# Attention and mixture-of-experts kernel: the scheduler's clock of a unit's row steps is moved on by one microsecond ahead of their transposes

## The chip, the cores and the metric

The kernel runs on one core of a Trainium2 chip. The metric is the device time of one execution in microseconds (us). The engines are TensorE (PE, with PEld for its weight loads), VectorE (DVE), ScalarE (ACT), GpSimd (POOL) and SyncE (SP), which here does nothing but issue transfers.

## The reference

Two layers follow each other. The first is a local attention over 7 taps with weights from a softmax; its output, 8 x 3584 = 28672 tokens of 192 numbers, goes into a layer with 8 experts of which each token takes one:

```python
w = exp(w - max(w)); w = w / (sum(w) + 1e-9)          # over the 7 taps, 8 heads
out[b, s, h] = sum_k w[b, s, h, k] * x_pad[b, s + k, h]   # x shifted by 0 to 6 tokens

logits = x @ w_gate                                   # x: 28672 x 192
e_idx = argmax(logits, axis=1)
gate_w = softmax(logits)[n, e_idx]
eom = sigmoid(x @ w_output_gate)
for e in range(8):
    h = maximum(x[mask_e] @ w1[e], 0)                 # 192 -> 1024
    out[mask_e] = gate_w * eom[:, e] * (h @ w2[e])    # 1024 -> 192
```

## The kernel before

The tokens are cut into 32 *units* of 896 (a batch has four; 128 partitions with 7 tokens each). A unit goes through a front:

- SP loads its weights `w` and its tokens `x` (for the first unit of a batch also the `halo`, the tokens shifted). There are four buffers for x.
- POOL and DVE multiply the taps (`gap`, `vt`), DVE adds them up.
- `sum_steps` turns the sums into rows `rt` in two half-precision parts (high and low), on ACT and DVE. There are three such row buffers.
- SP issues seven DMA transposes that turn `rt` into `gt`, the only buffer of its kind.
- PE multiplies `gt` by the gate's weights `gm` (21 small matmuls, "the logits"). DVE reduces them (`lz`), finds each token's expert (`eq`, `fm`) and counts with a scan (`p3`). PE turns that into ranks with two small matmuls, `p3` by `upper` and by ones. DVE works out each row's place `posi`.
- POOL scatters the rows by indirect DMA to their places in a table `srtd` in memory, sorted by expert (seven issues, `srtd<-rt,posi`).

As soon as an expert has enough rows, *tiles* are cut from the table: T0 to T75, with 512, 384, 256 or 128 rows of one expert. `round_steps` makes the list of tiles of each unit (tile 42 is one of unit 25), and from unit 31 on the remaining tiles are mixed by size. For each tile SP issues five loads (`tile_load`): `meta`, the transposed rows `xT`, two pieces of `wa` (the first layer's weights) and `wb` (the second's). A load that reads `srtd` waits for the scatters of all units up to its own. Then PE runs gemm1, five matmuls for each of its units of 512 columns (`ps<-xT,wa`), ACT makes `hh` (the high half of the activations), DVE `hl` (the low half), PE runs gemm2 for each group of 128 rows, 24 matmuls (`ps<-wb,hh` and `ps<-wb,hl`), ACT scales into `ys`, and POOL scatters `ys` to the output (`out_dram<-ys,meta`).

The order on each engine is fixed when the program is built, by a planner. Each step sequence, such as a unit's `sum_steps` or the loads of a tile, is a `Chain` with a reckoned time `c.t`: the earliest time at which its next instruction can start. `Order.step` always takes the chain whose start would be earliest, the latest of three times:

```python
at = max(self.now, c.t - c.slack, c.engine.t - c.engine.lead)
key = (at - c.favour, c.rank)
```

Between equal times the rank decides. The engines are modelled by `Paced` (each instruction moves the engine's clock and the chain's time by a cost and a latency) and the SP queue by `Queue`. The planner's times only set the order: on the chip every engine works through its own list and waits by semaphores. An instruction that waits holds up what stands behind it on the same engine, the SP queue too.

The steps that the change touches are in `sum_steps`, behind the split of the rows: from unit 5 on (`TR_U`), the chain takes the one buffer `gt`, issues the transposes on the queue `TQ` (SP), and goes on with the logits. The tile loads compete with these transposes for the places in SP's list.

Of the kernel before, what the change touches and what calls it, by code (L numbers as in the profile page):

```python
# [48 lines left out]
def SIZES(u, last):  # L49

    if last:
        return ((512, 0), (256, 0), (128, 0))
    return EARLY.get(u, ((512, 0),))

# [178 lines left out]
def kernel(ctx: ExitStack, tc: tile.TileContext, x, wg, wgate, wogate, w1, w2, cst, out):  # L233
    nc = tc.nc
    od = Order()
# [38 lines left out]
    def take(slots, engine):  # L274

        yield engine, lambda: slots
        got = slots.pop(0)
        od.cur.t = max(od.cur.t, got[0] if isinstance(got, tuple) else got)
        yield engine
        return got  # L280

    def take_place(slots):

        yield T_, lambda: slots or ("banks" in state and bank_free)
        got = slots.pop(0) if slots else (*bank_free.pop(0), bank_free)
        od.cur.t = max(od.cur.t, got[0])
        yield T_
        return got[1], got[2] if len(got) > 2 else slots
# [146 lines left out]
    def scales(ssq, sc, inv, name, free=None):  # L435

        n = ssq.shape[1]
        ex = f_ex if n == 2 else sp.tile([P, n], I32, tag=f"ex{n}", name=f"ex_{name}")
        V.tensor_scalar(ex, ssq.bitcast(I32), 1, MASK, op0=ALU.arith_shift_right, op1=ALU.bitwise_and)
        if free is not None:  # L440
            free.append(od.cur.t)
        yield V
        V.tensor_scalar(sc.bitcast(I32), ex, -1.0, float(197 << 23), op0=ALU.mult, op1=ALU.add)
        V.tensor_scalar(inv.bitcast(I32), ex, float(57 << 23), None, op0=ALU.add)
# [198 lines left out]
    def acc_steps(u, taps):  # L643
# [8 lines left out]
        while own or left:  # L652
# [25 lines left out]
            first = acc  # L678
        d["total"] = acc
        od.add(sum_steps(u), (RANK_B, u), S)  # L680

    def used(u, tag):
# [32 lines left out]
    def sum_steps(u):  # L715

        d = U[u]
        _, ri = yield from take(rt_free, S)
        d["ri"], rt = ri, ri.bitcast(F16)
        ssq = sp.tile([P, 1], F32, tag="ssq", name=f"ssq{u}")  # L720
        a3 = d["total"].rearrange("p (j h) g -> p j (h g)", h=H)

        b, q = u // UB, u % UB
        S.activation(ri[:, :, 192:194], tok.unsqueeze(2).broadcast_to([P, JS, 2]), AF.Copy, bias=float(b * SEQ + q * JS))
        S.activation(rt.bitcast(BF16)[:, :, 0:D], a3, AF.Square, accum_out=ssq)
        yield V
        sx = sp.tile([P, 1], F32, tag="sx", name=f"sx{u}")
        isx = d["isx"] = sp.tile([P, 1], F32, tag="isx", name=f"isx{u}")
        yield from scales(ssq, sx, isx, f"x{u}")
        yield S  # L730
        S.activation(rt[:, :, 0:D], a3, AF.Copy, scale=sx)
        yield V
        V.scalar_tensor_tensor(out=rt[:, :, 192:256], in0=a3[:, :, 128:192], scalar=sx, in1=rt[:, :, 128:192], op0=ALU.mult, op1=ALU.subtract)
        yield V
        V.scalar_tensor_tensor(out=rt[:, :, 256:384], in0=a3[:, :, 0:128], scalar=sx, in1=rt[:, :, 0:128], op0=ALU.mult, op1=ALU.subtract)
        d["split"] = True
        if u >= PE_U:
            acc_free.append(od.cur.t)
        else:
            sum_free.append((od.cur.t, d["sum_at"]))  # L740
        if u >= TR_U:
            yield from take(gt_free, TQ)
            gt = rp.tile([P, JS, 3, P], F16, tag="gt", bufs=GT, name=f"gt{u}")
            for j in range(JS):
                TQ.dma_start_transpose(out=gt[:, j], in_=rt[:, j, 0:384])
        yield S, lambda: "isg" in gates
        for k in ("isl", "nisl"):
            d[k] = sp.tile([P, 1], F32, tag=k, name=f"{k}{u}")
            S.activation(d[k], isx, AF.Copy, scale=gates[k[:-1] + "g"])
        yield T_  # L750
        at, home = yield from take_place(lg_free)
        lg = ps[:, at : at + 224].rearrange("p (j c) -> p j c", c=32)
        if u < TR_U:
            yield from pe_logits(u, rt, lg)
        else:
            od.cur.t += LAT_T
            for j0 in range(0, JS, 2):
                yield T_
                for j in range(j0, min(j0 + 2, JS)):
                    logits(lg, j, gt[:, j].rearrange("p k r -> p (k r)"))  # L760
            gt_free.append(od.cur.t)

        lz = d["lz"] = sp.tile([P, JS, 16], F32, tag="lz", name=f"lz{u}")
        yield V
        V.tensor_reduce(out=lz, in_=lg.rearrange("p j (h c) -> p j c h", h=2), axis=AX, op=ALU.add)
        home.append((od.cur.t, at))
        yield V

        l8 = lz[:, :, 0:8]
        yield from take(few_free, V)  # L770
        m = f_m
        V.tensor_reduce(out=m, in_=l8, axis=AX, op=ALU.max)
        yield V
        eq = sp.tile([P, JS, 8], F32, tag="eq", name=f"eq{u}")
        mb = m.unsqueeze(2).broadcast_to([P, JS, 8])
        V.tensor_tensor(out=l8, in0=l8, in1=mb, op=ALU.subtract)
        ex = d["ex"] = sp.tile([P, JS, 8], F32, tag="exl", name=f"exl{u}")
        od.add(exp_steps(u, ex, l8), (RANK_B, u), S)
        yield V
        V.scalar_tensor_tensor(out=eq, in0=l8, scalar=0.0, in1=e8b, op0=ALU.is_equal, op1=ALU.mult)  # L780
        yield V
        fm = sp.tile([P, JS], F32, tag="fm", name=f"fm{u}")
        V.tensor_reduce(out=fm, in_=eq, axis=AX, op=ALU.min)
        yield V
        ohe = f_oh
        oh = d["oh"] = ohe.rearrange("p e j -> p j e")
        V.tensor_tensor(out=oh, in0=e8b, in1=fm.unsqueeze(2).broadcast_to([P, JS, 8]), op=ALU.is_equal)
        yield V

        p3e = sp.tile([P, 8, JS], F16, tag="p3", name=f"p3_{u}")  # L790
        p3 = d["p3"] = p3e.rearrange("p e j -> p j e")
        V.tensor_tensor_scan(out=p3e.rearrange("p e j -> p (e j)"), data0=segs, data1=ohe.rearrange("p e j -> p (e j)"), initial=0.0, op0=ALU.mult, op1=ALU.add)
        od.cur.t += LAT_R
        yield T_
        d["rk_at"], d["rk_home"] = yield from take_place(rk_free)
        rk = d["rk"] = ps[:, d["rk_at"] : d["rk_at"] + 16]
        T_.matmul(rk[:, 0:8], lhsT=upper, rhs=p3[:, JS - 1, :], start=True, stop=True)
        T_.matmul(rk[:, 8:16], lhsT=ones16, rhs=p3[:, JS - 1, :], start=True, stop=True)
        od.add(weight_of_steps(u), (RANK_C, u, 1), V, V.t)
        od.add(place_steps(u), (RANK_C, u, 0), V)  # L800

    def logits(lg, j, gx):
        for k, m in enumerate(gates["mm"]):
            T_.matmul(lg[:, j, :], lhsT=gx[:, k * P : (k + 1) * P], rhs=m, start=(k == 0), stop=(k == 2), skip_group_check=True)

    def pe_logits(u, rt, lg):

        gx = None
        yield from take(gt_free, S)
        gt = rp.tile([P, JS, 3, P], F16, tag="gt", bufs=GT, name=f"gt{u}").rearrange("p j k r -> p j (k r)")  # L810
        for g0 in range(0, JS + 2, 2):
            for g in range(2):
                j = g0 - 2 + g
                if gx is not None and j < JS:
                    logits(lg, j, gt[:, j])
            ng = min(2, JS - g0)
            if ng > 0:
                yield from take(tr_free, T_)
                pt = turn
                for g in range(ng):  # L820
                    for k in range(3):
                        T_.transpose(out=pt[:, g * 384 + k * 128 : g * 384 + (k + 1) * 128], in_=rt[:, g0 + g, k * 128 : (k + 1) * 128], identity=ident)
                yield S
                gx = True
                S.copy(gt[:, g0 : g0 + ng, 0:384], pt[:, 0 : ng * 384].rearrange("p (j c) -> p j c", c=384))
                tr_free.append(od.cur.t)
                yield T_
        gt_free.append(od.cur.t)
        U[u]["turned"] = True

    def exp_steps(u, ex, l8):
        S.activation(ex, l8, AF.Exp, scale=U[u]["isl"])
        U[u]["exp"] = True
        U[u]["exp_t"] = od.cur.t
        return
        yield
# [314 lines left out]
    def last_turn_steps():  # L1151

        yield T_, lambda: state["weights"] == NE and "turned" in U[TR_U - 1]
        yield from take(tr_free, T_)
# [166 lines left out]
TURN_SP = True  # L1321
GT = 1
TR_U = 5
EARLY = {2: ((256, 0),), 4: ((384, 0),), 5: ((384, 0),), 6: ((384, 0),)}
EVERY = {*range(99)}
MANUAL = ("SP", "DVE", "PE", "Activation", "Pool")
# [18 lines left out]
```

## Time and the profile before

| | |
|---|---|
| median of 3 runs | 1253.18 us |
| lowest and highest | 1252.49 and 1254.74 us |
| profiled execution | 1240.45 us |
| its span in the trace | 1238.7 us |
| mean granted clock of PE | 0.985 |
| idle time of PE | 107.5 us (52.4 up to 300 us, 46.9 from 300 to 1000, 0.8 from 1000 to 1200, the rest at the end) |

The span is what the trace covers; the profiled execution is 1.7 us longer than it, and 12.7 us shorter than the median of the runs without a profile. A row of the timeline has the start and the duration in us, the engine, the source line, the operation with output and inputs and their shapes, and a count where equal instructions that follow each other are put together; in brackets stands the time that the engine stood idle before it and what ended that. Line 167 and line 139 are those of helpers through which every instruction goes, so all compute instructions show L167 and all issues of SP L139. The names in rows lack the numbers of units and tiles; which unit a row belongs to comes from its place in the order.

### The profile page before, as it was taken

The page shows a single profiled execution, that of the slowest core. Times are in us where ns is not written, and L with a number is a line of the kernel's source. Part 1 is how long each engine was busy: PE and PEld are TensorE (multiplying, and loading weights), DVE is VectorE, ACT ScalarE, POOL GpSimd, SP SyncE. Part 2 cuts the span into 40 slices and gives each one's busy share as a digit, 9 for nine tenths or more (in the row PEclk, how much of TensorE's full clock was granted, in tenths as well). Part 3 has the DMA queues.
Part 4 walks back from the last instruction along what each step waited for, and adds up shares of the span by engine and source line. Part 5 has one row for each costly group of instructions (what it writes and reads, how often), then busy time and mean ns, then how long its engine had stood idle before and what let it go on. Part 6 is the DMA issues. An engine that isn't in the chain of part 4 may idle for free.

```text
span 1238.7 us, 27551 instructions
## 1 busy us (share of the span) xinstructions
PE 1131.2 (91%) x9692; PEld 816.7 (66%) x9692; DVE 950.8 (77%) x2011; ACT 583.9 (47%) x1253; POOL 855.6 (69%) x759
## 2 busy tenths in 40 slices
PE   8987788798989999999999999999999999999997
PEld 4443357666666666766666666666666666888987
DVE  6787959988899899988988989989988753333331
ACT  2865634454444445544444544445444433444442
POOL 6676787886777888888878878878878654322222
PEclk9998899999999999999999999999999999999999
DMA  9885699799996787787857885986977496889991
GB/s 300 270 262 179 225 262 232 210 273 245 248 254 167 229 207 195 214 238 222 232 172 206 220 222 161 252 220 175 230 196 209 136 243 201 236 256 298 311 300 57
DMA packets 279404, 277.61 MB, mean 224 GB/s; under 512 B 213670, under 2 KB 238743, under 8 KB 279264
## 3 DMA queue, kind: packets, MB, share of 16 engines
q1 hardware_dynamic: 257424, 231.25, 67.8%
q0 software_dynamic: 21696, 44.30, 12.4%
q8 instruction: 76, 1.25, 0.4%
q14 instruction: 64, 0.52, 0.1%
q10 hardware_dynamic: 144, 0.29, 0.1%
HBM read 174.87 MB, written 60.28 MB: 190 GB/s over the span
## 4 chain that ended last, share of the span: by engine, by line
PE 54%; DVE 20%; issue 9%; POOL 6%; DMA 3%; SPq 2%; ACT 1%; another core or an unknown queue 1%; DVEq 0%; POOLq 0%; ACTq 0%
PE ps L167 54%; DVE ps L167 9%; DVE hl L167 5%; POOL gap L167 2%; POOL srtd L167 2%; SPq L139 1%; DVE vt L167 1%; DVE rt L167 1%; POOL out_dram L167 1%; DMA wb<-wd 1%; DMA wa<-wd 1%; DVE vap L167 1%; ACT hh L167 1%; DVE lz L167 0%
## 5 line engine op out<-in xcount | busy, mean ns | idle before, releaser
L167 PE MATMUL ps<-xT,wa 128*128 128x512 f16 (+3 forms) x2440 | 489.2, 347 | 32.9 <-DVE hl L167 13.6
L167 PE MATMUL ps<-wb,hh 128*128 128x192 f16 x3648 | 473.8, 247 | 13.8 <-issue 7.0
L167 PE MATMUL ps<-wb,hl 128*128 128x192 f16 x1824 | 450.6, 247 | 2.6 <-issue 2.6
L167 DVE SCALAR_TENSOR_TENSOR hl<-ps,hh 128x512 f16<-128x512 f32 (+1 forms) x470 | 306.1, 664 | 181.8 <-ACT hh L167 123.7
L167 POOL DMA_INDIRECT out_dram<-ys,meta x220 | 218.3, 992 | 235.1 <-ACT ys L167 174.5
L167 POOL TENSOR_TENSOR gap<-x,w 128x768 f32<-128x768 f32 (+5 forms) x251 | 343.4, 1392 | 38.6 <-PE ps L167 13.8
L167 PEld LDWEIGHTS <-wa 128*128 128x128 f16 x2440 | 226.7, 98 | 216.8 <-issue 44.8
L167 PEld LDWEIGHTS <-hh 128*128 128x128 f16 x3648 | 332.0, 98 | 54.9 <-issue 18.4
L167 ACT ACTIVATE hh<-ps 128x512 f16<-128x512 f32 (+1 forms) x470 | 269.3, 582 | 183.5 <-PE ps L167 151.4
L167 POOL DMA_INDIRECT srtd<-rt,posi x224 | 223.3, 997 | 80.3 <-issue 60.2
L167 ACT ACTIVATE ys<-ps,sc 128x192 f32<-128x192 f32 x228 | 95.6, 419 | 302.4 <-PE ps L167 188.1
L167 PEld LDWEIGHTS <-hl 128*128 128x128 f16 x1824 | 179.2, 98 | 3.8 <-issue 3.5
L167 DVE TENSOR_TENSOR ps<-ps,gap 128x1344 f32<-128x1344 f32 x116 | 179.8, 1550 | 0.7 <-POOL gap L167 0.4
L167 PE MATMUL ps<-gap,cf 128*128 128x512 f32 x168 | 72.9, 573 | 7.5 <-DVE ps L167 4.9
L167 POOL TENSOR_TENSOR gap<-halo,w 128x1152 f32<-128x1152 f32 (+4 forms) x37 | 59.4, 1606 | 17.2 <-PE ps L167 8.4
L167 DVE SCALAR_TENSOR_TENSOR rt<-ps,sx,rt 128x448 f16<-128x448 f32 x64 | 57.4, 909 | 10.2 <-ACT rt L167 3.1
L167 PE MATMUL ps<-vap,cf 128*128 128x512 f32 (+1 forms) x126 | 56.3, 583 | 3.4 <-DVE vap L167 3.4
L167 PEld LDWEIGHTS ps<-gap,cf 128*128 128x128 f32 x168 | 31.8, 201 | 39.2 <-issue 30.6
L167 DVE TENSOR_TENSOR vt<-x,ps 128x1344 f32<-128x1344 f32 (+2 forms) x42 | 52.7, 1269 | 0.2
L167 DVE TENSOR_TENSOR ps<-ps,vt 128x1344 f32<-128x1344 f32 x34 | 52.8, 1552 | 0.0
L167 PE MATMUL ps<-xT,late 128*128 128x128 f16 (+2 forms) x560 | 52.1, 250 | 0.5 <-issue 0.5
L167 ACT ACTIVATE rt<-ps,sx 128x1344 f16<-128x1344 f32 x32 | 44.0, 1375 | 10.7 <-DVE isx L167 5.4
(125 smaller groups left out, 815.0 us busy)
## 6 DMA issues: line engine op xcount, KB each, us to landing
wb<-wd SPq DMA_DIRECT2D x75, 768.5 KB
wa<-wd SPq DMA_DIRECT2D x61, 768.0 KB
x<-in_x_dram SPq DMA_DIRECT2D x32, 672.0 KB
late<-wd SPq DMA_DIRECT2D x14, 768.0 KB
wa<-wd SPq DMA_DIRECT2D x61, 128.0 KB
w<-in_wg_dram SPq DMA_DIRECT2D x32, 196.0 KB
wd<-wpb SPq DMA_DIRECT2D x8, 768.5 KB
st<-in_w_dram SPq DMA_DIRECT2D x8, 768.0 KB
```

Source lines behind the costliest of these rows:

```text
L139: r = f(*args, **kwargs)
L167: r = f(*args, **kwargs)
```

## The change

When a chain of `sum_steps` (unit 5 or later) has split its rows, its reckoned time is put 1.0 us later before it asks for the `gt` buffer and issues the transposes. The later steps of the same chain (scales on ACT, logits, ranks) are reckoned from that time too. A chain that competes for SP, the loads of a tile or of the next unit's tokens, comes first in SP's list if its time lies within that microsecond.

```diff
         if u >= TR_U:
+            od.cur.t += TURN_LAG
             yield from take(gt_free, TQ)
             gt = rp.tile([P, JS, 3, P], F16, tag="gt", bufs=GT, name=f"gt{u}")
             for j in range(JS):
                 TQ.dma_start_transpose(out=gt[:, j], in_=rt[:, j, 0:384])
...
 TR_U = 5
+TURN_LAG = 1.0
```

The number of instructions stays the same on every engine. The lists of PE, DVE and POOL are word for word the same (but for running numbers of buffers) for units 13 to 23; they differ in two stretches, about units 9 to 12 and units 24 to 31.

The first stretch begins on SP at the transposes of unit 9 (`gt9`). In these rows `w12`, `x12` and `halo` are the loads of unit 12, `ti6_0` is the list of unit 6's tiles, and `meta10` the first load of tile 10. Before:

```order
L139 DMA x11_3223<-in_x_dram 128x1344
L139 DMA w12_3272<-in_wg_dram 128x392
L139 DMA_TRANSPOSE gt9_3278<-rt_0_99 128x3x128 x7
L139 TENSOR_LOAD ti6_0_2421
L139 ISA x2
L1043 ISA
L139 DMA meta10_3441<-srtd_78 128x3x2
```

And after:

```order
L139 DMA x11_3223<-in_x_dram 128x1344
L139 DMA w12_3272<-in_wg_dram 128x392
L139 DMA halo_83<-in_x_dram 112x1152
L139 DMA halo_83<-in_x_dram 15x1152
L139 DMA x12_3280<-in_x_dram 128x1344
L139 DMA_TRANSPOSE gt9_3344<-rt_0_99 128x3x128 x7
L139 TENSOR_LOAD ti6_0_2421
```

The three loads of unit 12 have moved from behind tile 11's loads to ahead of `gt9`. On PE the logits of unit 9 have moved behind 34 more matmuls (ten of gemm1 of tile 9, 24 of gemm2 of tile 8), while the rank matmuls of unit 9 stand where they stood; those of unit 10 stand 29 matmuls later.

The second stretch shows first on DVE and PE at the ranks of unit 25. On DVE, `eq25`, `fm25` and `p3_25` are the search for the expert and the scan, `w27` and `w28` belong to the softmax of later units, and `hl38_0` is the low half of the first gemm1 unit of tile 38. Before:

```order
L167 TENSOR_TENSOR lz25_11751<-lz25_11751,ps_82 128x7x8
L167 TENSOR_TENSOR w27_10818<-w27_10818,ps_82 128x56x5
L167 SCALAR_TENSOR_TENSOR eq25_11814<-lz25_11751,ps_82 128x56
L167 TENSOR_TENSOR ps_82<-w27_10818,ps_82 128x112
L167 TENSOR_REDUCE fm25_11846<-eq25_11814 128x7
L167 TENSOR_REDUCE ps_82<-w28_11254 128x56
L167 TENSOR_TENSOR ps_82<-ps_82,fm25_11846 128x7x8
L167 TENSOR_TENSOR w28_11254<-w28_11254,ps_82 128x392
L167 SCALAR_TENSOR_TENSOR p3_25_11855<-segs_133,ps_82 128x56
L167 TENSOR_SCALAR ex_x26_11860<-ssq26_11807 128x1
L167 SCALAR_TENSOR_TENSOR hl38_0_11789<-ps_82,hh38_0_11788 128x512
```

And after:

```order
L167 TENSOR_TENSOR w27_10818<-w27_10818,ps_82 128x56x5
L167 TENSOR_TENSOR lz25_11750<-lz25_11750,ps_82 128x7x8
L167 SCALAR_TENSOR_TENSOR hl38_0_11789<-ps_82,hh38_0_11788 128x512
L167 SCALAR_TENSOR_TENSOR eq25_11816<-lz25_11750,ps_82 128x56
L167 TENSOR_TENSOR ps_82<-w27_10818,ps_82 128x112
L167 TENSOR_REDUCE fm25_11848<-eq25_11816 128x7
L167 TENSOR_REDUCE ps_82<-w28_11255 128x56
L167 TENSOR_TENSOR ps_82<-ps_82,fm25_11848 128x7x8
L167 TENSOR_TENSOR w28_11255<-w28_11255,ps_82 128x392
L167 SCALAR_TENSOR_TENSOR p3_25_11864<-segs_133,ps_82 128x56
```

`hl38_0` has moved ahead of the seven operations from `eq25` to `p3_25`. On PE the two rank matmuls of unit 25 have moved behind five more gemm1 matmuls of tile 38 and now stand in front of a gemm2 group of tile 37, not in the middle of tile 38's pair. The rank matmuls of unit 30 have moved in the same way, behind 34 matmuls: from the middle of a pair of gemm1 units of tile 46 to the middle of a pair of tile 47.

The third place is SP at the transposes of unit 27 (`gt27`). `x30` is the load of unit 30, `ti25_0` the list of unit 25's tiles, and `meta42`, `xT42`, `wa2` and `wb42` are the loads of tile 42. Before:

```order
L139 DMA x30_12292<-in_x_dram 128x1344
L139 DMA_TRANSPOSE gt27_12436<-rt_0_99 128x3x128 x7
L139 TENSOR_LOAD ti25_0_11989
L139 ISA x2
L1043 ISA
L139 DMA meta42_12594<-srtd_78 128x4x2
L139 ISA
L139 DMA_TRANSPOSE xT42_12596<-srtd_78 128x3x512
```

And after:

```order
L139 DMA meta42_12485<-srtd_78 128x4x2
L139 ISA
L139 DMA_TRANSPOSE xT42_12487<-srtd_78 128x3x512
L139 ISA
L139 DMA wa2_140<-wd_79 128x1536
L139 ISA
L139 DMA wa2_140<-wd_79 64x512
L139 ISA
L139 DMA wb42_12491<-wd_79 128x1537
L139 DMA_TRANSPOSE gt27_12593<-rt_0_99 128x3x128 x7
```

All five loads of tile 42 have moved ahead of `gt27`; in the same way those of tile 43 have moved ahead of the loads `w31` and `x31`, and those of tile 49 ahead of `gt31`. On PE the logits of unit 27 stand 68 matmuls later (48 of gemm2, 20 of gemm1), those of unit 29 58 later and those of unit 31 78 later. Among the tiles cut after the last unit, the sizes follow each other in another order: tile 52 is now one of 512 rows of unit 30 instead of one of unit 31's small ones; the number of 128-row blocks is the same.

## The prediction

> **What bounds the kernel now.** I read the page's engine line first, then windows of 50 us, and last the waits of the whole run, because a change of order can only pay where an engine waits.
>
> ```profile
> span 1238.7 us, 27551 instructions
> PE 1131.2 (91%) x9692; PEld 816.7 (66%) x9692; DVE 950.8 (77%) x2011; ACT 583.9 (47%) x1253; POOL 855.6 (69%) x759
> ```
>
> TensorE (PE) is busy for 1131.2 of 1238.7 us. So 107.5 us of PE idle time are all that a better order could take, with the little that half clock adds. The next rows are windows (length, then busy time of PE, PEld, DVE, ACT and POOL, then the granted clock, the DMA share and GB/s).
>
> ```profile
> 300.00:350.00 50.00, 46.67 (x404) 34.01 (x403) 45.68 (x111) 24.92 (x59) 38.08 (x33) 0.99 1.10 260
> 800.00:850.00 50.00, 45.63 (x388) 32.46 (x388) 43.12 (x78) 23.37 (x52) 40.41 (x37) 0.97 0.77 205
> 950.00:1000.00 50.00, 45.71 (x386) 31.91 (x385) 35.78 (x76) 22.26 (x51) 32.93 (x32) 1.00 0.51 135
> 1100.00:1150.00 50.00, 50.00 (x558) 43.31 (x557) 16.50 (x25) 20.84 (x44) 11.72 (x12) 1.00 0.94 264
> ```
>
> The front (units and tiles side by side) leaves PE 3 to 4 us idle in each 50, the late tiles none: 50.00 of 50.00. So the end is PE's work plus PE's waits in the front, and a microsecond of PE wait saved at 300 or 820 us is a microsecond off the end. The permutation that the change makes of the late 512-, 256- and 128-row tiles is costed at 0: the same 128-row blocks are computed, and PE is full there. The waits (total, times, longest) say who is late:
>
> ```profile
> PE ps L167 <- issue: 26.3, 35, 4.1
> PE ps L167 <- DVE hl L167: 17.2, 25, 2.2
> SPq L139 <- DVE rt L167: 116.9, 16, 16.6
> ```
>
> SyncE's queue stands 116.9 us waiting for rows to transpose, so it has room. Putting a load ahead of such a wait is free as long as the load itself needs nothing that is later than the rows.
>
> **The change, part by part.** Nothing is added or removed on any engine. The instructions of units 13 to 23 keep their order on PE, DVE and POOL (a few small ACT scalings go one slot later), so all effects come from units 9 to 12 and 24 to 31.
>
> *Place 1, SyncE at gt9.* Halo and x of unit 12 go out ahead of the transposes of unit 9's rows instead of after tile 11's weights. On PE the ten gemm1 matmuls of tile 9 and the gemm2 group of tile 8 that followed the logits of unit 9 now stand before them, while the rank matmuls of unit 9 keep their place.
>
> ```profile
> 271.01 0.38 SPq L139 DMA_DIRECT2D w<-in_wg_dram  x1
> 276.66 9.77 SPq L139 DMA_TRANSPOSE gt<-rt  x7
> 299.44 1.00 SPq L139 DMA_DIRECT2D halo<-in_x_dram  x2
> 300.49 0.36 SPq L139 DMA_DIRECT2D x<-in_x_dram  x1
> 299.05 0.76 PE L167 MATMUL ps<-gm,gt 128*128 128x32 f16 x21
> 303.83 0.98 PE L167 MATMUL ps<-xT,wa 128*128 128x384 f16 x5
> 305.06 1.79 PE L167 MATMUL ps<-xT,wa 128*128 128x384 f16 x10 [0.25 <-DVE hl L167]
> 306.68 0.17 PE L167 MATMUL ps<-p,upper 128*128 128x8 f16 x1
> ```
>
> SyncE sits from 271.39 to 276.66 (5.3 us); the three issues take about 1.4 us, so they cost SyncE nothing. Their bytes may delay gt9 by a few us, but its issue ends at 286.43 and the logits run at 299.05, now later: no cost. On PE the logits now end where the row at 303.83 begins. DVE can then start lz of unit 9 at about 304.2 and needs some 2.8 us to the end of the scan (an estimate: seven short operations at about 0.26, as the two in the rows for unit 25 below, and two longer ones between them at about 0.5, as the half of the hh row there), so the rank matmuls at 306.68 would start at about 307.1: +0.4. The wait of 0.25 for a bank goes, as that DVE work comes earlier. Together **+0.2**; ends −0.25 and +2.2 (the longest wait for DVE in the list).
>
> *Place 2, the ranks of unit 25.* They go behind five more gemm1 matmuls of tile 38, and on DVE hl of tile 38's first bank goes from behind the scan that makes p3_25 to ahead of eq25.
>
> ```profile
> 818.06 1.24 PE L167 MATMUL ps<-xT,wa 128*128 128x512 f16 x5
> 821.47 0.17 PE L167 MATMUL ps<-p,upper 128*128 128x8 f16 x1 [2.17 <-DVE hl L167]
> 822.07 1.33 PE L167 MATMUL ps<-xT,wa 128*128 128x512 f16 x5 [0.40 <-DVE hl L167]
> 818.72 1.07 ACT L167 ACTIVATE hh<-ps 128x512 f16<-128x512 f32 x2
> 818.85 0.28 DVE L167 TENSOR_TENSOR ps<-w,ps 128x112 f32<-128x112 f32 x1 [1.77 <-ACT rt L167]
> 820.52 0.26 DVE L167 TENSOR_TENSOR_SCAN p<-segs,ps 128x56 f16<-128x56 f16 x1
> 820.74 1.28 DVE L167 SCALAR_TENSOR_TENSOR hl<-ps,hh 128x512 f16<-128x512 f32 x2
> 819.30:823.10 3.80, 1.23 (x8) 0.61 (x7) 3.63 (x17) 2.64 (x8) 3.60 (x4) 1.00 0.94 201
> 823.10:826.50 3.40, 3.40 (x22) 3.14 (x21) 3.14 (x14) 2.28 (x4) 2.09 (x2) 0.50 0.99 337
> ```
>
> Now PE ends its five matmuls at 819.30 and waits 2.17 and then 0.40: 2.57 of 3.80 us idle. After the change ACT's first hh ends at about 819.25 (half of the row's 1.07), hl follows in 0.64 and frees the bank at 819.9; the next five matmuls run to 821.1; DVE has then spent eq (0.2, by its neighbours) and the stretch 818.85 to 820.78, 1.93 us, and the scan ends at about 822.0. PE waits 0.6 and 0.9, together 1.5 instead of 2.57: **−1.1**. Ends: 0 (hl comes no earlier, since hh does not) and −2.57.
>
> The last row is the second cost of that wait: 3.40 us at a granted clock of 0.50, so 1.7 us of PE work lost. The nearest shorter gap without it is this one, after which the clock stayed whole:
>
> ```profile
> 947.01 0.17 PE L167 MATMUL ps<-p,upper 128*128 128x8 f16 x1 [1.71 <-ACT ys L167]
> ```
>
> With 1.5 us idle the place falls on the side of the 1.71, so I take **−1.7**; ends 0 and −1.7. [...]
>
> *Place 3, the ranks of unit 30.* They go from the middle of tile 46's pair to behind a gemm2 group and five more matmuls, 34 in all.
>
> ```profile
> 978.10 0.17 PE L167 MATMUL ps<-p,upper 128*128 128x8 f16 x1 [0.76 <-DVE sx L167]
> 978.80 1.24 PE L167 MATMUL ps<-xT,wa 128*128 128x512 f16 x5 [0.50 <-DVE hl L167]
> 867.40:871.54 4.14, 4.14 (x35) 2.95 (x34) 4.14 (x6) 1.37 (x4) 3.66 (x5) 1.00 0.70 139
> ```
>
> Ten gemm1 and 24 gemm2 matmuls take 4.14 us, as the third row shows for such a stretch of 34. That covers the 0.76 five times over. The 0.50 waits for a bank and comes back wherever DVE's hl is late; I leave it. **−0.8**; ends 0 and −1.26.
>
> *Place 4, SyncE at gt27 and gt31.* Tile 42's five loads go ahead of gt27, and tile 49's ahead of gt31. The logits of unit 27 move behind 48 gemm2 and 20 gemm1 matmuls, by the stretch above 2 x 4.14 = 8.28 us.
>
> ```profile
> 848.64 0.44 SPq L139 DMA_DIRECT2D x<-in_x_dram  x1
> 853.76 0.98 POOL L167 DMA_INDIRECT srtd<-rt,posi  x1 [0.30 <-issue]
> 856.36 9.62 SPq L139 DMA_TRANSPOSE gt<-rt  x7
> 867.37 0.42 SPq L139 DMA_DIRECT2D meta<-srtd  x1
> 871.24 0.41 SPq L139 DMA_DIRECT2D wb<-wd  x1
> 871.54 0.68 PE L167 MATMUL ps<-gm,gt 128*128 128x32 f16 x21
> 589.66 0.98 POOL L167 DMA_INDIRECT srtd<-rt,posi  x1 [0.30 <-issue]
> 595.69 0.40 SPq L139 DMA_DIRECT2D meta<-srtd  x1
> ```
>
> Tile 42 holds rows of unit 25, so its loads wait for that unit's last scatter, which POOL ends issuing at 854.74. At 595.69 a tile load that waited for the scatter of 589.66 came 5.05 us after the scatter's issue ended; so tile 42's loads start at about 859.8 instead of 867.37, take their 4.3 us (867.37 to 871.65), and gt27 starts at 864.1 instead of 856.36, 7.7 us late. Its issue ends at about 873.7. Now it ends at 865.98 and the logits at 871.54 do not wait, so it needs at most 5.6 us to land: 879.3 at the latest, against a new slot of 871.54 + 8.28 = 879.8. **0**, but with a cover of half a microsecond if landing takes all of those 5.6 us. The rank matmuls of units 27 and 29 come closer behind their logits; they had no wait for DVE, and I take 0 there too.
>
> The sum is +0.2 − 1.1 − 1.7 − 0.8 = −3.4 us. The profiled execution took 1240.45 us (span 1238.7) and would take 1237.0; it lies 12.7 us, 1.0%, below the median of 1253.18, and I carry the difference over: **1249.8 us**.
>
> **The rivals.**
>
> [...]
>
> 2. *Clearly faster.* The longest wait goes too:
>
> ```profile
> 296.30 0.33 PE L167 MATMUL ps<-wb,hh 128*128 128x192 f16 x2 [4.11 <-issue]
> ```
>
> It ends 2.75 us ahead of the logits of unit 9, in the middle of the reordered stretch. If moving unit 12's loads from 299 to 272 us changes what delays it, 4.1 us go, and with them a half-clock stretch like that at 823 (1.7). Against it: the loads moved come after this wait, and nothing on PE before it is reordered. Time: 1249.8 − 5.8 = 1244.0.
>
> 3. *Slower.* gt27 comes after its slot. Tile 42's transposes may not issue in 1.5 us as now; the row for tile 12's shows what they can take behind other loads:
>
> ```profile
> 302.80 10.18 SPq L139 DMA_TRANSPOSE xT<-srtd  x1
> ```
>
> With 10.2 us there, gt27 is 8.7 us later still, and PE waits some 8 us at unit 27's logits with half clock after it. The cover of 0.5 us (by the upper bound; more if landing is quicker) is where it begins to cost, and from about 4.2 us of stall, with 1.7 us of clock, the kernel is over 0.2% slower. For it: SyncE has a true dependence in front of gt27 now. Against it: around 860 us the queue carries no big load, the last one having gone out at 848.64. Time: 1256.5 at some 5 us of stall and the clock's 1.7 us, up to 1260.
>
> **How the numbers follow.** A measurement of this kernel can tell about 0.2%, 2.5 us, from no change; so faster means below 1250.7 and slower above 1255.7. The forecast has a chance of 0.40, its own range 1248 to 1252; a fifth of it (0.08) ends above 1250.7. Rival 1 has 0.28, rival 2 0.12, rival 3 0.20. Faster is 0.32 + 0.12 = 0.44, no change 0.28 + 0.08 = 0.36, slower 0.20. The range goes from rival 2's 1244.0 to rival 3's 1256.5, and leaves out the longer stalls of both.
>
> **What would show it.** Right: the rank matmuls of unit 25 wait under 1 us, and the windows behind them have a clock of 1.00; the rank matmuls of unit 30 don't wait; the logits of unit 27 follow gemm1 without a wait, though gt27 starts near 864; SyncE's three loads for unit 12 stand at 271 to 276 us. Wrong: a wait of PE at the logits of unit 27 or 31 for SyncE's transposes; a half-clock stretch at another place of the front; the wait of 4.1 us at 292 gone or doubled. What would upset the forecast most is that PE's unnamed waits (26.3 us) settle anew when the order changes.

## The result, and the profile after

| | before | after |
|---|---|---|
| median | 1251.91 us (11 runs, 1244.71 to 1255.13) | 1258.61 us (11 runs, 1255.28 to 1266.29) |
| span of the profiled execution | 1238.7 us | 1253.5 us |

The ratio is 1.0059, with a 95% interval of 1.0037 to 1.0081: the change makes the kernel slower by about 0.6%, where 0.3% faster was forecast. A second comparison gave 1.0029 (1.0004 to 1.0055). The two put the loss at 0.6% and 0.3%, 7 and 4 us, and their intervals reach from 0.04% to 0.8%. Executions of one kernel lie up to 1.5% apart (with units from 16 on, below: 1248.06 to 1266.19 us); three in a slow state, of 1265.02, 1270.52 and 1930.99 us, are in no ratio. In the traces of this case a good part of that stands where PE's list is the same in all kernels: up to the ranks of unit 8 they take from 271 to 280 us, and from the 3000th to the 5438th matmul from 303 to 312 us. So totals of two traces aren't compared below, but stretches that hold the same matmuls.

The page after, its engine line:

```profile
span 1253.5 us, 27530 instructions
PE 1140.6 (91%) x9692; PEld 818.1 (65%) x9692; DVE 951.4 (76%) x2011; ACT 582.6 (46%) x1253; POOL 854.3 (68%) x759
```

PE is busy 9.4 us longer with the same matmuls, and its idle time is 112.9 us instead of 107.5. The longer busy time is half clock: from 280 us to the end of the late tiles this trace has eight times 3.41 us at half clock, the trace before three times. Most of that isn't the change's doing. Four of the eight lie between 367 and 729 us, where PE's list is the same, and the traces of the seven other kernels below with the old order at units 24 to 27 have five to nine. The execution profiled before was a lucky one. The windows of 50 us (columns as in the prediction) show the loss thinly spread:

```profile
900.00:950.00 50.00, 45.55 (x366) 31.43 (x365) 42.05 (x91) 21.55 (x49) 36.34 (x34) 0.93 0.57 150
1150.00:1200.00 50.00, 49.04 (x588) 43.41 (x585) 16.60 (x24) 20.41 (x43) 11.46 (x12) 1.00 1.06 310
```

The first row has a granted clock of 0.93, and the second, in the tail, is not full. What happened is plainest in PE's waits in the late front, 790 to 1040 us (total, times, longest). Before:

```profile
PE ps L167 <- ACT ys L167: 6.8, 5, 1.9
PE ps L167 <- issue: 4.6, 9, 1.0
PE ps L167 <- DVE hl L167: 3.8, 4, 2.2
PE ps L167 <- DVE sx L167: 0.8, 1, 0.8
PE ps L167 <- DVE lz L167: 0.5, 1, 0.5
```

After:

```profile
PE ps L167 <- issue: 9.6, 17, 2.1
PE ps L167 <- DVE hl L167: 2.7, 4, 1.1
PE ps L167 <- ACT ys L167: 2.4, 2, 1.9
PE ps L167 <- DVE sx L167: 2.2, 1, 2.2
```

Waits for ACT and DVE fell from 11.9 to 7.3 us, and waits without a named engine ("issue") rose from 4.6 to 9.6. Most of the fall is in waits for ACT (6.8 to 2.4), which the forecast had not counted on. The other traces show the same exchange. From the 5523rd to the 7359th matmul the six traces with the front reordered from unit 24 on have 7.6 to 10.8 us of unnamed waits, and the seven with the old order at units 24 to 27 have 3.5 to 6.5 (without the kernel whose loads are doubled, below). On the mean the unnamed waits rose from 4.9 to 9.2 us and the named ones fell from 11.8 to 7.2, so almost nothing is left of the gain.

The same matmuls, before and after, in windows of PE alone (length, PE busy, clock, DMA share, GB/s). First the 6441st to the 6560th matmul, then the 6561st to the 7359th, then from the 7601st to the last. Before:

```profile
901.39:915.88 14.49, 12.61 (x121) 1.00 1.09 294
915.88:1016.15 100.27, 93.13 (x802) 1.00 0.66 180
1045.78:1231.01 185.23, 184.74 (x2094) 1.00 0.84 245
```

After:

```profile
911.01:931.10 20.09, 15.64 (x121) 0.83 0.92 262
931.10:1029.22 98.12, 93.32 (x802) 1.00 0.68 176
1060.05:1245.85 185.80, 184.84 (x2094) 1.00 0.83 243
```

The first stretch takes 5.6 us more, the second 2.2 less, the tail 0.6 more. The experiments give each kernel's trace of these stretches.

### The profile page after: what moved, and what is told of

Same layout as the page of the kernel before. It is cut to its first block, busy times and chain, and to the rows that moved or that the text cites. A ratio compares the mean times of both kernels' runs of the same rounds, so it can differ in the third digit from the quotient of the medians.

```text
span 1253.5 us, 27530 instructions
## 1 busy us (share of the span) xinstructions
PE 1140.6 (91%) x9692; PEld 818.1 (65%) x9692; DVE 951.4 (76%) x2011; ACT 582.6 (46%) x1253; POOL 854.3 (68%) x759
## 3 DMA queue, kind: packets, MB, share of 16 engines
q8 instruction: 76, 1.25, 0.4%
## 4 chain that ended last, share of the span: by engine, by line
PE 55%; DVE 22%; issue 8%; DMA 3%; ACT 3%; SPq 2%; another core or an unknown queue 2%; POOL 1%; DVEq 0%; POOLq 0%; ACTq 0%
PE ps L167 55%; DVE ps L167 10%; DVE hl L167 5%; DVE rt L167 2%; SPq L139 2%; DMA x<-in_x_dram 1%; DVE vt L167 1%; POOL gap L167 1%; DMA out_dram<-ys,meta 1%; ACT hh L167 1%; ACT rt L167 1%; DMA wa<-wd 1%; DVE w L167 1%; DVE lz L167 1%
## 5 line engine op out<-in xcount | busy, mean ns | idle before, releaser
L167 PE MATMUL ps<-xT,late 128*128 128x128 f16 (+2 forms) x560 | 59.0, 261 | 1.0 <-DMA late<-wd 1.0
L167 PEld LDWEIGHTS <-late 128*128 128x128 f16 x560 | 39.9, 98 | 13.6 <-DMA late<-wd 1.7
## 6 DMA issues: line engine op xcount, KB each, us to landing
wb<-wd SPq DMA_DIRECT2D x75, 768.5 KB
wa<-wd SPq DMA_DIRECT2D x61, 768.0 KB
late<-wd SPq DMA_DIRECT2D x14, 768.0 KB
wa<-wd SPq DMA_DIRECT2D x61, 128.0 KB
wd<-wpb SPq DMA_DIRECT2D x8, 768.5 KB
st<-in_w_dram SPq DMA_DIRECT2D x8, 768.0 KB
```

Of the source, the lines that this page charges most:

```text
L167: r = f(*args, **kwargs)
```

## The experiments

Adding the microsecond only for some units splits the change: for units below 16 it gives exactly the early stretch of the new order, for units from 16 on exactly the late one, tail included.

```diff
-            od.cur.t += TURN_LAG
+            od.cur.t += TURN_LAG if u < 16 else 0.0
```

> The microsecond is added for units below 16 alone. The order is then that of the changed kernel in units 9 to 12 and that of the kernel before everywhere else. Theory 1, the early stretch costs (in the trace after, tile 13 begins 4.1 us later than before, and the ranks of unit 10 wait 1.33 us for DVE behind the logits): 1256 us, slower by 0.3%. Theory 2, the late stretch costs everything: 1252, no change.

Measured: 0.9991 (0.9963 to 1.0019). The early stretch costs nothing that can be measured.

With `u >= 16` instead:

> The microsecond is added for units 16 and up alone: the order of the kernel before up to unit 12, that of the changed kernel from unit 24 to the end. Theory 1, the early stretch costs 4 of the 7 us: 1255. Theory 2, the late stretch costs everything (in the trace after, tile 44 begins 14.2 us late where tile 42 began 9.5 late, and the ranks of unit 25 still wait 2.16 us with half clock behind them): 1258.5. If both stretches only hand the loss to waits that move from run to run, neither part alone is slower than 1254.

Measured: 1.0033 (0.9998 to 1.0068), median 1259.19 us against 1253.83. The loss lies with the late stretch, as the early one alone has none, though this interval still touches 1.

With `u == 24`, which reorders the late front but not the tail:

> The microsecond is added for unit 24 alone. That moves tile 42 ahead of the transposes of unit 27 and reorders DVE and PE from the ranks of unit 25 to about tile 47, but leaves the order of the tiles behind unit 31 as before. Theory 2 with the cause at units 25 to 27: as slow as the late stretch whole, 1257 to 1259. If the cause lies in units 28 to 31 or in the tail's order: 1252.

Measured: 1.0001 (0.9968 to 1.0033). In its trace a gain and a loss stand against each other: the wait for the ranks of unit 25 is gone (the 5761st to the 6060th matmul take 36.3 us, in kernels with the old order 37.6 to 39.7), and a run of unnamed waits at 948 to 954 us, which no trace of the old order has at those matmuls, takes it back (the 6561st to the 6900th take 48.2 us, in those kernels 42.7 to 45.2; without the doubled loads). Tile 42 goes ahead of `gt27` here too, yet the 6441st to the 6560th matmul take 13.5 us, no more than in the old order. So that swap alone doesn't slow this stretch.

The tail alone, on the kernel before:

```diff
-            queue[:] = mixed(queue)
+            queue[:] = queue[:1] + mixed(queue[1:])
```

> The kernel before with one edit: the last 512-row tile of unit 30 is taken out of the mixing of the late tiles and put in front. From there to the end the tiles then follow each other as in the changed kernel, and nothing ahead of it moves. The forecast had this at 0. Theory 3, the tail's order costs (the trace after shows one wait of 0.96 us for late weights at 1179, where the trace before has none): 1253, slower by 0.1%. Otherwise 1252.

Measured: 1.0017 (0.9986 to 1.0048); undecided by time. The trace has the wait again (PE's waits, 1060 to 1240 us):

```profile
PE ps L167 <- DMA late<-wd: 1.3, 1, 1.3
```

The changed kernel once more:

> The changed kernel once more, beside the next three on the same chip. 1.003 to 1.008 times the kernel before by the first runs. Its profile again has a wait for late weights of about 1 us or more near 1180 us, if that wait belongs to the tail's order and not to that one execution.

Measured: 1.0029 (1.0004 to 1.0055). The wait for late weights is there, 2.2 us. All four traces with the new tail have it (1.0, 2.2, 2.8 and 1.3 us). From the 7601st matmul to the last they take 185.8, 188.5, 189.2 and 186.1 us; eight of the nine traces with the old tail take 184.5 to 185.4, the ninth, of the next kernel, 187.2.

The changed kernel with the old tail (the 512-row tiles are spread as if one more of them were left):

```diff
-        keyed.append(((k - (1.0 if f[0] == 512 else 0.5 if f[0] == 256 else 0.0)) / n[f[0]], f))
+        keyed.append((k / (n[f[0]] + 1) if f[0] == 512 else (k - (0.5 if f[0] == 256 else 0.0)) / n[f[0]], f))
```

> The changed kernel, but the late tiles are mixed so that from tile 52 on they follow each other as before the change; everything up to there is the changed kernel's order. Theory 3, the tail's order carries a part of the loss: about 3 us faster than the changed kernel (1.001 to 1.003 times the kernel before), and no wait for late weights behind 1070 us. If the loss is all in units 24 to 31: as slow as the changed kernel.

Measured: 1.0033 (1.0002 to 1.0065), no better than the changed kernel beside it. Its trace also has two short waits for late weights (0.7 and 0.5 us, at 1146 us) and 187.2 us for the tail. So the expected 3 us did not show, and the old order does not rule the wait out. Why it came here and not with units 16 to 26 and the old tail (below), whose rows come as late (the last scatter at 1046.7 us, here at 1044.1), these traces don't tell.

Units 28 to 31 alone:

> The microsecond is added for units 28 to 31 alone: the logits and ranks of units 29 and 31 move on PE, DVE and ACT, SyncE's list stays as before, and so does the tail. If the later logits cost by themselves (the four profiles have 131.6 to 132.9 us from the 6335th to the 7360th matmul with the late stretch changed, 127.8 to 130.6 without): 2 to 3 us slower, 1.002. If SyncE's order or the tail costs: no change, 0.999 to 1.001.

Measured: 1.0031 (1.0002 to 1.0060). Taken apart further, the two halves of it:

> The microsecond is added for units 28 to 30 alone. One thing moves on PE: the 21 logit matmuls of unit 29 go behind one more gemm2 group, and on DVE the scan of that unit a few places back; SyncE's list does not change. If the loss of the version with units 28 to 31 (1.0031) hangs on unit 29's logits: 1.002 to 1.003. If on unit 31's or on nothing but chance: 0.999 to 1.001.

Measured: 1.0000 (0.9975 to 1.0025).

> The microsecond is added for unit 31 alone: ten gemm1 matmuls of a tile go ahead of the logits of unit 31, and its ranks move by ten matmuls. If the loss of the version with units 28 to 31 hangs on unit 31 (its profile has two waits of 0.68 and 0.85 us and half clock behind them at 1036 us): 1.002 to 1.003. Otherwise 0.999 to 1.001.

Measured: 1.0004 (0.9977 to 1.0031). The two parts don't add up to the whole, whose interval nearly touches 1: that loss was chance, or a meeting of both that these runs don't tell.

Units 16 to 26 with the old tail:

> The microsecond is added for units 16 to 26, and the late tiles are mixed as before the change. It has tile 42 ahead of gt27, tile 49 ahead of gt31 and the later logits of unit 27, but not the moved logits of unit 29 that come from units 28 to 30. If SyncE's reordering carries the loss: 1.003, with a stretch of about 19 us and 4 us of PE waits from the 6441st to the 6561st matmul, where the old order takes 14 to 15 with 2. If the units behind 27 carry it: 1.000 and about 14.5 us there.

Measured: 1.0004 (0.9983 to 1.0026). The stretch of 120 matmuls takes 19.1 us as expected, but the next 800 take 98.2 us where kernels with the old order take 100.1 to 103.8: much of the loss is given back. The stretch came as the first branch expected, the time as the second.

Two experiments test the mechanisms by making them larger. All large tiles of the mixing first:

```diff
-        keyed.append(((k - (1.0 if f[0] == 512 else 0.5 if f[0] == 256 else 0.0)) / n[f[0]], f))
+        keyed.append((0.0 if f[0] == 512 else (k - (0.5 if f[0] == 256 else 0.0)) / n[f[0]], f))
```

> The kernel before, but all 512-row tiles that are left at the mixing run first and the small ones follow in one stretch. Theory 3 says that PE waits for weights where many small tiles follow each other without a large one between, since each tile loads 1.66 MB whatever its size: waits for weights of 3 to 10 us in the last 130 us, 1.003 to 1.008 times the kernel before. If the wait near 1180 us has another cause: no wait for weights, and no change.

Measured: 1.0079 (1.0045 to 1.0113), with these waits of PE in 1060 to 1240 us:

```profile
PE ps L167 <- DMA wa<-wd: 6.0, 4, 2.5
PE ps L167 <- DMA late<-wd: 2.9, 3, 1.7
```

8.9 us of waits for weights, within the 3 to 10 expected: the order of the tiles can set the time, and the tail is not full by itself.

And more load traffic in the late front (the second copy is issued past the planner, so that no other list moves):

```diff
         SP.dma_start(out=wb, in_=wd[bass.ds(e, 1), :, 2048:WW].rearrange("a p c -> p (a c)"))
+        if 40 <= t <= 47:
+            SP.engine.dma_start(out=wb, in_=wd[bass.ds(e, 1), :, 2048:WW].rearrange("a p c -> p (a c)"))
```

> The kernel before, in which SyncE loads wb of tiles 40 to 47 twice, one copy behind the other: 0.77 MB more for each, 6.1 MB in all between 800 and 960 us, nothing else moved. Theory 4, PE's waits without a named engine come where a tile's load and a scatter of rows share the DMA engines: at least 4 us more of such waits from the 5523rd to the 7360th matmul, and 1.002 to 1.006. If they come from DVE and ACT: no more of them and 0.999 to 1.001, since a tile's load has 20 us and more until its first use.

Measured: 1.0041 (1.0008 to 1.0073). PE's waits, 790 to 1040 us:

```profile
PE ps L167 <- issue: 8.0, 16, 1.9
PE ps L167 <- ACT ys L167: 4.1, 3, 2.0
PE ps L167 <- DVE hl L167: 4.0, 5, 2.0
PE ps L167 <- DMA gt<-rt: 2.9, 5, 1.1
```

Unnamed waits rise to 8.0 us, from 4.6 in the kernel before and 6.0 in the version above, whose front is the old one; the expected 4 us more are not reached. From the 5523rd to the 7359th matmul they are 7.6 us, above the 3.5 to 6.5 of the seven others with the old order. The 2.9 us for `gt<-rt` come from SyncE's list, where the second copies stand ahead of transposes. The time is in the expected range, for two reasons instead of one.

## Why the prediction was wrong, point by point

Two kinds of steps failed. In the sum, the wait at place 2 was reckoned 0.7 us too short, and with it the clock term was gone in the profile after. Outside the sum, place 4 and the order of the late tiles stood at 0. By the traces they cost 4.7 us in one stretch, behind which 2.8 came back, and 2.3 us in the tail. The forecast counted the named waits that would go and none that would come.

**Place 1** was near: the logits of unit 9 and the rank matmuls behind them, after:

```profile
304.32 0.68 PE L167 MATMUL ps<-gm,gt 128*128 128x32 f16 x21
307.92 0.17 PE L167 MATMUL ps<-p,upper 128*128 128x8 f16 x1 [0.47 <-DVE p L167]
```

+0.4 was expected for that wait, 0.47 came. In SyncE's rows the three loads stand at 271.23 to 276.90, and the transposes start at 277.07 instead of 276.66, so they were free as forecast; the transposes take 12.12 us to issue instead of 9.77 and still end ahead of the logits. Alone, the early stretch measures 0.9991.

**Rival 2's wait** went, though its time did not come. In the trace before, 4.11 us stood in front of the 1552nd matmul. All ten traces with the old early order have 3.5 to 5.3 us there (in nine of them named as a wait for ACT's ys), and none of the four with the new one has more than 0.5 at that matmul. Shorter waits came behind it, in the trace after 1.12 us without a named engine at 296.41 and 1.65 us for DVE's hl at 299.04. The 1301st to the 1957th matmul take 81.3 to 84.9 us with the new early order and 79.9 to 84.9 with the old. So the condition of rival 2 came true and no time was saved by it.

**Place 2** failed in the profile after: −1.1 and −1.7 were expected. The idle time fell by 0.4, and half clock followed again.

```profile
825.88 2.41 PE L167 MATMUL ps<-xT,wa 128*128 128x512 f16 x10
830.45 0.17 PE L167 MATMUL ps<-p,upper 128*128 128x8 f16 x1 [2.16 <-DVE sx L167]
825.36 0.42 ACT L167 ACTIVATE ys<-ps,sc 128x192 f32<-128x192 f32 x1 [5.59 <-PE ps L167]
826.30 0.69 DVE L167 SCALAR_TENSOR_TENSOR hl<-ps,hh 128x512 f16<-128x512 f32 x1 [1.58 <-ACT hh L167]
827.82 0.29 DVE L167 TENSOR_TENSOR ps<-w,ps 128x112 f32<-128x112 f32 x1 [0.71 <-ACT rt L167]
829.49 0.26 DVE L167 TENSOR_TENSOR_SCAN p<-segs,ps 128x56 f16<-128x56 f16 x1
829.71 0.68 DVE L167 SCALAR_TENSOR_TENSOR hl<-ps,hh 128x512 f16<-128x512 f32 x1
```

PE does its ten gemm1 matmuls without a wait for a bank, where 0.6 us was expected: ACT now does tile 38's first hh ahead of the square of the rows, so hh ends 0.4 us behind the start of these matmuls (826.27 against 825.88) and not 1.2. The scan came as reckoned: it ends 3.87 us behind that start, 3.94 by the sum. But the sum lets the rank matmuls start as the scan ends, and they start 0.70 us later, as DVE's next hl ends (829.71 + 0.68; the row names `sx`, but in the trace before `sx` came only at 821.94, behind the rank matmul). The rows of the prediction show the same: the scan ended at 820.78, the first of the two hl at about 821.4, and the rank matmul started at 821.47 with a wait named for hl. Wherever else the rank matmuls of a unit from 3 on wait over 0.3 us in this trace, they start 0.05 or 0.06 us behind their scan. With these 0.70 us the sum would have given 3.94 + 0.70 − 2.41 for the ten matmuls, 2.2 us of idle time instead of 1.5. 2.16 came, and this was no longer on the side of the 1.71.

The scan itself hangs on ACT: DVE's `ps<-w` waits for the square of the rows, both before (818.85) and after (827.82). With the late stretch alone the same order had 0.57 us at these ranks, as the square ended 2.1 us ahead of PE's ten matmuls instead of 0.5, and with unit 24 alone there was no wait of 0.4 us or more. So the size varies with when ACT comes to it. Over the five traces with this order the idle time at these matmuls is 0.6 (twice) and 2.0 to 2.2 (three times), and in the eight with the old order 2.3 to 2.6. Half clock follows in one of the five and in five of the eight. The 5779th to the 5814th matmul take 6.3 us on the mean where the old order takes 8.2. So over all traces about 1.9 of the forecast 2.8 us came; in the one profile after, little.

Behind the wait the clock falls again:

```profile
830.48:833.24 2.76, 2.76 (x27) 0.71 1.04 321
833.24:836.30 3.06, 3.06 (x12) 0.70 0.59 225
```

So a wait of 2.16 us in one piece, with PE busy on both sides of it, was followed by half clock. The prediction's measure, the length of the wait, isn't the right one. A wait of 1.52 us was followed by half clock (it ends at 443.30 us in the trace with unit 24 alone) and one of 3.14 us was not (at 366.29 in that of the changed kernel with the old tail). In each of the 14 traces the changes of the clock lie on one grid of 3.41 us, in the traces before and after to within 0.01 us. Of the grid's windows at full clock between 284 and 1040 us, 43 were idle for 0.60 of their length or more, and half clock followed each; it followed none that was idle for less than 0.41. Two windows of the grid in the trace after, each with the one behind it (length, PE busy, clock, DMA share, GB/s):

```profile
828.24:831.66 3.42, 1.26 (x18) 1.00 1.09 331
831.66:835.07 3.41, 3.41 (x17) 0.50 0.94 305
807.76:811.17 3.41, 1.48 (x11) 1.00 0.89 241
811.17:814.58 3.41, 3.41 (x30) 1.00 0.48 100
```

The first holds the 2.16 us and was idle for 0.63 of its length, and half clock came behind it; the third was idle for 0.57, and none came. So in these traces the idle share of one window of the grid told half clock better than the length of a wait did, and between 0.41 and 0.60 it left both open: a term of −1.7 taken from one execution should have had the weight of a chance.

**Place 3** was right as to its wait: the rank matmuls of unit 30 stand without one.

```profile
996.91 0.17 PE L167 MATMUL ps<-p,upper 128*128 128x8 f16 x1
```

But two waits stand near it that the trace before lacks, 0.82 us for hl at 993.68 and 0.43 us for ys at 997.54, so nothing is left of the 0.8 there.

**Place 4** was right by its own steps and missed the cost. SyncE and PE after:

```profile
865.01 0.29 SPq L139 DMA_DIRECT2D meta<-srtd  x1
869.96 9.59 SPq L139 DMA_TRANSPOSE gt<-rt  x7
888.27 0.68 PE L167 MATMUL ps<-gm,gt 128*128 128x32 f16 x21
```

Transposes of unit 27 start 13.6 us later than before (PE itself was 8 us late by then), and the logits run at 888.27 without a wait for them. Rival 3 did not happen; that its 1256.5 us lies near the result is luck. What came was not in the sum: the ranks of unit 27 are later, its scatters come closer together on POOL, and they fall on tile 44's loads. PE, SyncE and POOL after, at the logits of unit 28:

```profile
913.48 0.68 PE L167 MATMUL ps<-gm,gt 128*128 128x32 f16 x21
914.79 0.24 PE L167 MATMUL ps<-wb,hl 128*128 128x192 f16 x1 [0.21 <-issue]
915.48 0.24 PE L167 MATMUL ps<-wb,hh 128*128 128x192 f16 x1 [0.44 <-issue]
916.21 0.24 PE L167 MATMUL ps<-wb,hh 128*128 128x192 f16 x1 [0.49 <-issue]
918.53 0.32 PE L167 MATMUL ps<-wb,hl 128*128 128x192 f16 x1 [2.07 <-issue]
911.00 1.30 SPq L139 DMA_DIRECT2D wa<-wd  x2
913.30 0.71 SPq L139 DMA_DIRECT2D wb<-wd  x1
910.70 0.97 POOL L167 DMA_INDIRECT srtd<-rt,posi  x1 [0.30 <-issue]
917.12 0.98 POOL L167 DMA_INDIRECT srtd<-rt,posi  x1 [0.30 <-issue]
```

And the windows of PE there:

```profile
914.34:918.50 4.16, 0.97 (x6) 0.82 0.98 358
918.50:924.00 5.50, 4.83 (x22) 0.52 1.15 252
```

For 4.2 us PE issues a matmul or two each 0.7 us, then it runs at half clock. The first and the last of five scatters stand there; the DMA engines are at 0.98. Before, the same matmuls ran through, though three scatters at 1.3 us from each other and loads of a tile (`xT` from 905.31, `wa` from 908.70) came in the same time:

```profile
905.15 0.68 PE L167 MATMUL ps<-gm,gt 128*128 128x32 f16 x21
901.33 0.98 POOL L167 DMA_INDIRECT srtd<-rt,posi  x1 [0.30 <-issue]
906.55 0.98 POOL L167 DMA_INDIRECT srtd<-rt,posi  x1 [0.30 <-issue]
907.83 0.98 POOL L167 DMA_INDIRECT srtd<-rt,posi  x1 [0.30 <-issue]
909.12 0.98 POOL L167 DMA_INDIRECT srtd<-rt,posi  x1 [0.30 <-issue]
```

From 905.15 to 909.98 us PE was busy for all of the 4.83 us, at a DMA share of 1.08, above that of the crawl. So close scatters and busy DMA engines aren't enough by themselves; what more it takes these rows don't show. All five traces of kernels with this part of the order have the crawl at these matmuls (18.9 to 20.1 us for the 120), and none of the seven with the old order (13.9 to 15.2). With unit 24 alone the crawl at 948 to 954 us has the same company: five scatters of unit 28 from 944.28 to 950.71 and issues of `wa` and `wb` from 944.77 to 949.16.

**The permutation of the late tiles** was costed at 0 and cost about 1 to 4 us by the traces of the four kernels that have it, in the profile after by this wait:

```profile
1179.36 0.39 PE L167 MATMUL ps<-xT,late 128*128 128x512 f16 x1 [0.96 <-DMA late<-wd]
```

"PE is full there" was read as "order can't matter". Every tile loads 1.66 MB, whatever its size (768.0, 128.0 and 768.5 KB on the page), and by the 4.14 us of 34 matmuls in the prediction PE uses one up in about 4 us for 128 rows and 16.6 for 512 (an estimate): if so, the order spreads the demand on the DMA engines. By time this cost isn't settled: the new tail alone is within its interval of 1, and taking it out of the changed kernel gained nothing.

Together, by the traces of stretches with the same matmuls (means of seven traces with the old order there against five with the new; unit 24 alone and the doubled loads are left out; for the tail nine against four, with these two): +4.7 us at the 120 matmuls, −2.8 in the 800 behind them, −0.7 in the 920 ahead (place 2's gain is in it), +2.3 in the tail, 3.4 in all. The ranges of the first two don't overlap between the orders, the second's barely; those of the 920 and of the tail do, and a stretch of 2439 matmuls with one order varies by 9 us, so the sum is rough. The timed runs say 4 to 7. The prediction's last sentence named the right thing, that the unnamed waits may settle anew, but not that a loss may come of it.

**What stays open**: what holds PE in the unnamed waits. In the 14 traces, from 280 to 1040 us, PE stood 0.089 us in each us in which both weights (`wa`, `wb`) and scatters of rows into `srtd` moved, 0.031 with scatters alone, 0.015 with weights alone, and 0.010 with neither (counted in half-microseconds from the transfers' records). This says where they come, not why; the doubled loads raised them, by less than expected. Another possible cause, the 16 KB instruction transfers (queue 8 of the page, 76 packets with 1.25 MB), finds no support in the records. Of 95 us of unnamed waits over 0.25 us from the 5523rd to the 7359th matmul in these traces, 4.5 us (5%) fall in time in which one of them moves, and such time is 7% of the whole. With unit 24 alone none moves between 943.1 and 963.6 us, through the whole crawl there. One that is late before its record begins would not show. Taking the scatters away from such a place was not tried. That their meeting with tile 44's loads causes the crawl is therefore argued, not shown. The division of the loss between front and tail isn't settled by time either, as each part alone is within its interval of 1 or barely out of it.

## What to carry to other kernels

When a planner's numbers move one queue's order, follow the move on all engines until the lists agree again; here the cost stands, by the traces, at a meeting of scatters and loads three steps further on, and in the order of tiles 150 us later. End a reckoned wait where the rows end it: here the matmul waited not for the scan but for the hl behind it, 0.7 us more. Before a term is taken from one profile, ask whether the next execution has it; the half clock behind this wait stood in five of eight traces. A named wait that goes can come back as another, so compare the whole stretch. An engine that is busy without a gap may still depend on its order, where the order sets how much must be loaded per microsecond: with the large tiles first PE waited 8.9 us for weights.

## What was not expected of the hardware

- PE has waits that follow no engine's work, steps of 0.7 us with a matmul or two in each (from 914.34 to 918.50 us in the trace after), and they came most often while weights and row scatters shared the DMA engines: 0.089 us per us against 0.010 with neither.
- Half clock came in stretches of 3.41 or 6.83 us on a fixed grid of 3.41 us, behind windows of that grid in which PE was idle for 0.41 of the time or more, and behind every one with 0.60 or more. A wait of 1.52 us was followed by it in one place, and one of 3.14 us was not in another.
- Twelve executions of one program lay 1.5% apart on the same chip (1248.06 to 1266.19 us, with units from 16 on). Kernels with the same order up to there differed by 9 us in the first 270 us, and by 9 us again in a later stretch that is the same in all.
